# An S4 convolution with a gated linear unit on one core: token normalisation and three copies on GpSimd, and a new written-out order

## Chip, core and metric

The kernel runs on one core of a Trainium2 chip. The metric is the device time in microseconds of one execution, median of the runs. Engines are named as in the profile: PE is TensorE (matrix products, with PEld its weight loads), DVE is VectorE, ACT is ScalarE, POOL is GpSimd, SP is SyncE, whose queue here only issues DMAs.

## What is computed

The input u has 2048 tokens of 512 channels, in bf16. It is normalised over the channels; the normalised xn goes through two branches, and u and both results are added.

```python
xn = (u - mean) / sqrt(var + 1e-5)            # per token, 512 channels
K  = real(einsum("dn,dnl,dn->dl", C, exp(dt * A * l), dt * B))   # 128 modes, l = 0 .. 2047
y  = irfft(rfft(pad(xn)) * rfft(pad(K))) + xn * Dskip            # long convolution over tokens
g  = (sigmoid(xn @ w_gate) * (xn @ w_up)) @ w_down               # 512 -> 1792 -> 512
out = u + y + g
```

## The kernel before

**Tiles and stages.** Tokens lie on 128 partitions, 16 tokens to a partition (index i, 0 to 15; "token" below means one such slice of 128 tokens by 512 channels). Channels are done in two halves b of 256. The gated unit works in eight groups of two tokens. Its stages for a group: the transposed input xnT, products with W into PSUM tiles pg and pu (L824), a sigmoid on ACT into hT (L881), a product on DVE (L883), and the down products po (L829).

**The normalisation** (`layernorm`, L449 on). DVE takes statistics per token (bn_stats, L454), in three batches: tokens 0 and 1, 2 and 3, and 4 to 15. For each batch it forms mean and variance, POOL takes the square root of the variance as a power (sd, L503), and DVE takes the reciprocal (rinv, L479) and the bias nb (L480). Each token is then normalised by one instruction: L483 on DVE, or L487 on ACT. Tokens 4 to 15 are all on ACT in the kernel before. Groups 0 and 1 are transposed by PE (L493) and copied out of PSUM; groups 2 to 7 by DMA transposes on SP's queue, one a token. The spectrum of xn (pzx, L787) needs all tokens.

**The convolution kernel K** is built without 2048 exponentials per mode. `params` computes the first exponentials of a half by exponential and sine at four time scales (ACT and DVE, tiles wp and wq, f32), squares them (L609 to L620), and copies them as bf16 into H and gm by four copies of 128x1024 (L622, here called the H and gm copies). `hlevels` then fills the 21 rows of H by complex products on DVE (L667 to L670, L683 to L686), and `level` fills the 32 rows of G by doubling: five levels, each of two products (L642 into a scratch tile tB, L643 into G) and two sums (L644, L645). All of that is DVE work with both operands in SBUF, done once per half for H and twice per half for G (a quarter of the channels each). PE multiplies G with H (pk, L729), ACT or DVE evicts to ks, and DMAs through scratch memory in HBM (kt_scr, then kf) spread K over time steps. The spectra of K (pzk, L807) and xn go through scratch as well (zk_scr, z_scr), are transformed (px, pkf, L952), multiplied (XX, L972 on DVE, either straight from PSUM or after an eviction by ACT, L973), and transformed back (pv, L961, v_scr; py, L1000).

**What sets the order.** Every step is a task of a plan with an engine, a planned duration in us and an optional alternative engine (`alt`). The order of all 919 tasks is written out as a tuple ORDER, the tasks that take their alternative as OTHER, and the PSUM buffer of each PSUM tile as SIDE. `emit` (L206 on) only follows these: an engine executes its tasks in the order of ORDER, and planned durations have no effect on the chip, except through the ORDER that was made with them. DMAs are issued by SP's queue or, by OTHER, by POOL's.

Of the kernel before, what the change touches and what calls it, by code (L numbers as in the profile page):

```python
# [13 lines left out]
ACT = mybir.ActivationFunctionType  # L14
# [15 lines left out]
ND = 256  # L30
# [187 lines left out]
class _Kernel:  # L218
# [230 lines left out]
    def layernorm(self):  # L449
        nc, add, s, xn = self.nc, self.p.add, self.small, self.xn  # L450
        v = nc.vector
# [30 lines left out]
        def norm(i):  # L482
            v.tensor_scalar(out=xn[:, i, :], in0=self.acc[:, i, :], scalar1=s["m_f"][:, i:i + 1], scalar2=s["rinv"][:, i:i + 1],  # L483
                            op0=ALU.subtract, op1=ALU.mult)

        def norm2(i):
            nc.scalar.activation(out=xn[:, i, :], in_=self.acc[:, i, :], func=ACT.Identity, scale=s["rinv"][:, i:i + 1],  # L487
                                 bias=s["nb"][:, i:i + 1])
# [10 lines left out]
        for lo, hi in ((0, 2), (2, 4), (4, 16)):  # L499
            rk = {0: 2, 2: 4, 4: 10}[lo]  # L500
# [3 lines left out]
                out=s["sd"][:, lo:hi], in0=s["ve"][:, lo:hi], in1=s["half"][:].to_broadcast([128, hi - lo]), op=ALU.pow), [r],  # L504
                    rk + 0.5 * (hi - lo))
            r = add("DVE", 0.4, lambda lo=lo, hi=hi: rstd(lo, hi), [r], rk + 0.5 * (hi - lo))
            for i in range(lo, hi):
                self.norm[i] = add("DVE", 0.4, lambda i=i: norm(i), [r], rk + 0.5 * (hi - lo) + 0.1 + 4 * max(0, i - lo - 3),
                                   alt=("ACT", 0.83, lambda i=i: norm2(i)) if i >= 2 else None)
        self.turns = []  # L510
        for g in range(NGRP):
            rk = max(3, 27 * g + 4)
            xT = self.sb([128, KT, GT * 128], "xnT", 4)
            self.xnT.append(xT)
            if g > 1:
# [7 lines left out]
                    take=[pt])  # L523
# [6 lines left out]
    def params(self, b):  # L530
        nc, add, s = self.nc, self.p.add, self.small
# [90 lines left out]
        cp = lambda o, i, **kw: A_(1.03, lambda: act(out=o(), in_=i(), func=ACT.Identity), **kw)  # L622
# [11 lines left out]
    def level(self, T, nq, n, m, after, rk, own):  # L634
# [6 lines left out]
        cost = lambda k: 0.085 + k * sz / 1920  # L641
# [4 lines left out]
        if n < 8:  # L646
            return [self.p.add("DVE", sum(cost(x[0]) for x in ops), lambda: [x[1]() for x in ops], after, rk, take=[tB], use=own)]
# [5 lines left out]
    def hlevels(self, b):  # L653
# [4 lines left out]
        def lv(src, dst, n, m, after, step=1, to=1, each=0):  # L658

            tB = self.sb([128, 2, 2048], "tB", 1)  # L660
            cost = 0.085 + n * ND / 1920
# [10 lines left out]
            return [self.p.add("DVE", 6 * cost - 0.17, go, after, rk, take=[tB], use=own)]  # L672
# [335 lines left out]
    def store(self):  # L1008
# [46 lines left out]
OTHER = (  # L1055
# [6 lines left out]
SIDE = ("03212320310203120132303322221230100130130221102302112132313110301233311013013232321031200130121323212010200021"  # L1062
        "2133132321331232320221202010301313131020021113202321231210120232030333311003002")
# [35 lines left out]
```

## Time and profile before

| | us |
|---|---|
| median of 3 runs | 237.17 (236.57 to 238.12) |
| the profiled execution | 236.26 |
| its span, first to last instruction | 234.5 |
| PE busy | 212.6 (91% of the span), 2149 matrix products |
| DVE busy | 203.8 (87%), 302 instructions |
| ACT busy | 170.3 (73%), 213 instructions |
| POOL busy | 49.1 (21%), 80 instructions |

All durations are of the one profiled execution. Lengths of neighbouring instructions overlap a little, so that a DVE product listed with 0.68 us advances its queue by about 0.60. The granted TensorE clock was 0.998 of full speed. Lines are those of the kernel before; in the changed file they are one further on from L509 up.

### The profile page before, as it was taken

To read this page: it belongs to the slowest core of one execution; us is meant where nothing else is said; L and a number is where in the kernel's file an instruction comes from. 1 tells how busy PE (TensorE), PEld (TensorE's weight loads), DVE (VectorE), ACT (ScalarE), POOL (GpSimd) and SP (SyncE) were. 2 spreads that over 40 slices of the span, in tenths; PEclk is the share of its full clock that TensorE was granted. 3 is DMA by queue.
4 is the path that set the end of the run, shared out by engine and by line. 5 is a ranking of instruction groups with operands and counts; after the bars stand their busy time and mean duration, and the time that the engine had idled before them with its cause. 6 is when DMAs were issued, how large, how long until landed. Compare 5 with 4: busy or idle time off the path is not lost.

```text
span 234.5 us, 5353 instructions
## 1 busy us (share of the span) xinstructions
PE 212.6 (91%) x2149; PEld 147.8 (63%) x2169; DVE 203.8 (87%) x302; ACT 170.3 (73%) x213; POOL 49.1 (21%) x80
## 2 busy tenths in 40 slices
PE   3798999987989979999989999999989995999993
PEld 1386887466568757564868489557656553677641
DVE  3999999899999999999999999369997789885672
ACT  3399999899989959983976184655888878784400
POOL 2400001400002100025002010562453432422031
PEclk9999999999999999999999999999999999999999
DMA  6999900405030530276996865499589997976946
GB/s 174 286 334 350 303 9 0 130 19 136 20 92 3 126 60 1 36 239 157 275 265 186 283 150 171 93 213 244 195 269 312 264 336 232 278 266 179 286 164 224
DMA packets 51963, 43.16 MB, mean 184 GB/s; under 512 B 20113, under 2 KB 44722, under 8 KB 51682
## 3 DMA queue, kind: packets, MB, share of 16 engines
q1 hardware_dynamic: 47218, 30.07, 45.9%
q0 software_dynamic: 4304, 12.54, 17.3%
q8 instruction: 17, 0.28, 0.5%
q10 hardware_dynamic: 416, 0.20, 0.3%
q14 instruction: 8, 0.07, 0.1%
HBM read 25.86 MB, written 15.37 MB: 176 GB/s over the span
## 4 chain that ended last, share of the span: by engine, by line
DVE 42%; PE 38%; ACT 8%; DMA 8%; issue 2%; POOL 1%; SPq 0%; ACTq 0%; DVEq 0%
PE po L829 9%; PE pg L824 8%; PE pu L824 6%; DVE tB L642 6%; DVE G L643 6%; DMA H<-z_scr 3%; DVE G L644 3%; PE pkf L952 3%; DVE G L645 3%; DMA G<-v_scr 3%; DVE stats L454 3%; PE pv L961 2%; PE py L1000 2%; PE pzk L807 2%; PE pk L729 2%
## 5 line engine op out<-in xcount | busy, mean ns | idle before, releaser
L824 PEld LDWEIGHTS <-W 128*128 128x128 bf16 x896 | 86.3, 98 | 22.6 <-issue 8.8
L824 PE MATMUL pg<-xnT,W 128*128 128x256 bf16 x504 | 61.3, 273 | 3.3 <-ACT hT L358 1.2
L824 PE MATMUL pu<-xnT,W 128*128 128x256 bf16 x392 | 47.6, 273 | 1.6 <-DVE xnT L359 1.3
L972 DVE TENSOR_TENSOR XX<-pkf,x 128x1024 bf16<-128x1024 f32 x22 | 26.4, 1221 | 7.9 <-PE pkf L952 4.6
L829 PE MATMUL po<-wd,hT 128*128 128x512 bf16 x134 | 31.4, 379 | 0.4 <-issue 0.2
L884 ACT ACTIVATE ub<-pu 128x1024 bf16<-128x1024 f32 x18 | 18.6, 1032 | 8.7 <-PE pu L824 5.7
L829 PEld LDWEIGHTS <-hT 128*128 128x128 bf16 x140 | 13.5, 98 | 15.6 <-issue 0.6
L881 ACT ACTIVATE hT<-pg 128x1024 bf16<-128x1024 f32 (+1 forms) x16 | 14.7, 917 | 10.9 <-PE pg L824 8.9
L642 DVE TENSOR_TENSOR tB<-G,gm 128x256 bf16<-128x256 bf16 (+4 forms) x20 | 19.6, 980 | 0.3 <-ACT G L704 0.2
L643 DVE TENSOR_TENSOR G<-G,gm 128x256 bf16<-128x256 bf16 (+4 forms) x20 | 19.6, 979 | 0.1
L358 ACT ACTIVATE zs<-pzx 128x1024 bf16<-128x1024 f32 x16 | 16.3, 1039 | 3.9 <-PE pzx L787 3.9
L1004 DVE TENSOR_TENSOR acc<-py,acc 128x1024 bf16<-128x1024 f32 x8 | 9.7, 1220 | 5.9 <-PE py L1000 5.9
L952 PEld LDWEIGHTS <-w 64*64 64x64 bf16 x384 | 9.2, 106 | 8.5 <-issue 4.9
L358 ACT ACTIVATE G<-pv 128x1024 bf16<-128x1024 f32 x13 | 13.1, 1028 | 1.4 <-PE pv L961 1.3
L454 DVE BATCH_NORM_STATS2 stats<-acc 128x6 f32<-128x512 bf16 x16 | 10.5, 682 | 4.0 <-DMA acc<-in_A_u_dram 4.0
L729 PE MATMUL pk<-H,G 128*128 128x84 bf16 x256 | 11.0, 199 | 3.2 <-DVE G L645 1.8
L729 PEld LDWEIGHTS <-G 128*128 128x128 bf16 x256 | 10.2, 96 | 4.6 <-DVE G L645 2.1
L350 POOL DMA_DIRECT2D kf<-kt_scr x14 | 7.8, 563 | 24.1 <-DMA kt_scr<-ks 22.3
L829 PE MATMUL po<-wd,hTb 128*128 128x512 bf16 x54 | 12.6, 379 | 0.1
L973 ACT ACTIVATE XX<-pkf 128x1024 bf16<-128x1024 f32 x10 | 10.1, 1021 | 3.4 <-PE pkf L952 3.4
L358 ACT ACTIVATE x<-px 128x1024 bf16<-128x1024 f32 x10 | 10.2, 1027 | 3.3 <-PE px L952 3.2
L350 POOL DMA_DIRECT2D kt_scr<-ks x5 | 3.7, 736 | 42.6 <-ACT ks L358 42.6
(146 smaller groups left out, 372.2 us busy)
## 6 DMA issues: line engine op xcount, KB each, us to landing
z_scr<-zs SPq DMA_DIRECT2D x13, 256.0 KB, 2.4
zk<-zk_scr SPq DMA_DIRECT2D x11, 256.0 KB, 4.7
v_scr<-G SPq DMA_DIRECT2D x9, 256.0 KB, 3.8
v_scr<-G POOLq DMA_DIRECT2D x7, 256.0 KB, 4.0
W<-in_B_w_up_dram SPq DMA_DIRECT2D x3, 512.0 KB, 5.7
acc<-in_A_u_dram SPq DMA_DIRECT2D x3, 512.0 KB, 8.9
W<-in_B_w_gate_dram SPq DMA_DIRECT2D x3, 512.0 KB, 9.6
zk_scr<-zks SPq DMA_DIRECT2D x6, 256.0 KB, 2.7
```

The costliest lines, as they stand in the source:

```text
L350: go = lambda e: lambda: q[e].dma_start(out=out(), in_=in_(), **(dict(transpose=True) if transpose else {}))
L358: return self.p.add("ACT", 0.17 + n / 1190, lambda: nc.scalar.activation(out=dst(), in_=src(), func=ACT.Identity), after, rank, alt=("DVE" ...
L454: v.bn_stats(out=s["stats"][:, i, :], in_=self.acc[:, i, :])
L642: ops = [(2, lambda: tt(out=tv(), in0=l, in1=mb(1), op=ALU.mult), [], [tB], []), (2, lambda: tt(out=o, in0=l, in1=mb(0), op=ALU.mult), [], ...
L643: (2, lambda: tt(out=o, in0=l, in1=mb(0), op=ALU.mult), [], [], []),
L729: nc.tensor.matmul(o, G[:, q, r].rearrange("p g c -> p (g c)"), H[:, r, :, 4 * (CQ * c + q):4 * (CQ * c + q) + 4], start=r == 0, stop=r == 1)
L824: nc.tensor.matmul(p[:, lo + n, :], W[:, i, kt, k * 128:(k + 1) * 128], xT[:, kt, :], start=kt == 0, stop=kt == KT - 1)
L829: nc.tensor.matmul(po[:, jj, :], hT[:, k, jj * 128:(jj + 1) * 128], wd[:, k, :], start=k == 0, stop=k == FT - 1 and self.outs[i // GT].eng ...
L881: e1 = add("ACT", 0.17 + n * 256 / 1190, lambda hk=hk, n=n, pg=pg: nc.scalar.activation(out=hk(), in_=pg[:, 0:n, :], func=ACT.Sigmoid), mg ...
L884: e2 = add("ACT", 0.17 + n * 256 / 1190, lambda uk=uk, pk=pk: nc.scalar.activation(out=uk(), in_=pk(), func=ACT.Identity), mu + [e1], rk + ...
L952: nc.tensor.matmul(p[o:o + 64, par, h, :], self.w3[i:i + 64, w, 64 * g:64 * g + 64], z[i:i + 64, 2 * h + c, :], start=True, stop=True, til ...
L972: prod = lambda xo=xo, x1=x1, src=None: nc.vector.tensor_tensor(out=xo(), in0=src(), in1=x1[:, 0], op=ALU.mult)
```

## The change

Three things in the code, and a new order.

Tokens 4 to 15 have POOL as their alternative instead of ACT, and all twelve take it. The four H and gm copies of each half get POOL as an alternative, and three of the eight take it: in the first half the H copy of wp, in the second half the H and the gm copy of wq. The planned durations of the G and H operations are set anew; these only enter the planner.

```diff
-        def norm(i):
-            v.tensor_scalar(out=xn[:, i, :], in0=self.acc[:, i, :], scalar1=s["m_f"][:, i:i + 1], scalar2=s["rinv"][:, i:i + 1],
+        def norm(i, e=v):
+            e.tensor_scalar(out=xn[:, i, :], in0=self.acc[:, i, :], scalar1=s["m_f"][:, i:i + 1], scalar2=s["rinv"][:, i:i + 1],
                             op0=ALU.subtract, op1=ALU.mult)
...
-                                   alt=("ACT", 0.83, lambda i=i: norm2(i)) if i >= 2 else None)
+                                   alt=("POOL", 0.9, lambda i=i: norm(i, nc.gpsimd)) if i >= 4 else ("ACT", 0.83, lambda i=i: norm2(i)) if i >= 2 else None)
...
-        cp = lambda o, i, **kw: A_(1.03, lambda: act(out=o(), in_=i(), func=ACT.Identity), **kw)
+        cp = lambda o, i, **kw: A_(1.03, lambda: act(out=o(), in_=i(), func=ACT.Identity),
+                                 alt=("POOL", 1.35, lambda: nc.gpsimd.tensor_copy(out=o(), in_=i())), **kw)
...
-        cost = lambda k: 0.085 + k * sz / 1920
+        cost = lambda k: 0.15 + k * sz / 1920
...
-            return [self.p.add("DVE", sum(cost(x[0]) for x in ops), lambda: [x[1]() for x in ops], after, rk, take=[tB], use=own)]
+            return [self.p.add("DVE", 0.49 + 6 * sz / 1920, lambda: [x[1]() for x in ops], after, rk, take=[tB], use=own)]
...
-            cost = 0.085 + n * ND / 1920
+            cost = 0.49 + 6 * n * ND / 1920
...
-            return [self.p.add("DVE", 6 * cost - 0.17, go, after, rk, take=[tB], use=own)]
+            return [self.p.add("DVE", cost, go, after, rk, take=[tB], use=own)]
...
 ORDER = (
...
 OTHER = (
...
 SIDE = (
```

ORDER, OTHER and SIDE are replaced as a whole. Read against the order before, the main differences are these. On POOL the first H copy stands ahead of the twelve-token power, then eleven norms with the load of Dskip among them, two issues of the ks dump, the twelfth norm and the two copies of the second half; POOL issues 68 DMAs instead of 63. On DVE the fourth G level of the first quarter comes ahead of the large H products of the first half (L683), where it came behind them; the two xnT copies of groups 0 and 1 go to ACT, the first of them behind three of the four exponentials; of the 32 XX products, 17 instead of 22 are taken straight from PSUM, and 15 instead of 10 after an eviction by ACT. In the frequency stage the issues of single z_scr, zk_scr and v_scr transfers are spread otherwise over SP and POOL. The matrix products on PE are the same, in an order that differs in places by some microseconds of work.

More of the change, by code (lines that the diff above doesn't have):

```diff
@@ L1014 @@
 ORDER = (
[40 rows of a table removed]
-OTHER = (
[6 rows of a table removed]
-SIDE = ("03212320310203120132303322221230100130130221102302112132313110301233311013013232321031200130121323212010200021"
-        "2133132321331232320221202010301313131020021113202321231210120232030333311003002")
[40 rows of a table added]
+OTHER = (
[6 rows of a table added]
+SIDE = ("00223310031202133211133201212012233113012333030201121231330032030211323001321203100021200130123310312021210303"
+        "1333303133203112112210231032302323132102231221212233021002311313003023210211003")
 @with_exitstack
```

92 rows, old and new, of tables (ORDER, OTHER) are left out of this document.

## The prediction

> **What bounds the kernel now.** I read the windows first, ten microseconds each: the window, then busy time of PE, PE weight loads, DVE, ACT and POOL (counts in brackets), then clock, DMA share and GB/s.
>
> ```profile
> 30.00:40.00 10.00, 9.95 (x89) 8.50 (x88) 9.83 (x30) 10.00 (x12) 0.00 (x0) 1.00 0.01 3
> 40.00:50.00 10.00, 9.21 (x50) 4.81 (x50) 9.12 (x17) 9.06 (x17) 3.83 (x3) 1.00 0.30 86
> 50.00:60.00 10.00, 8.73 (x78) 7.42 (x77) 9.90 (x15) 9.97 (x13) 0.00 (x0) 1.00 0.35 93
> 60.00:70.00 10.00, 9.36 (x95) 5.36 (x95) 9.90 (x15) 9.25 (x18) 0.00 (x0) 1.00 0.21 54
> 190.00:200.00 10.00, 7.43 (x165) 4.57 (x167) 9.43 (x11) 8.68 (x10) 2.36 (x5) 1.00 0.84 257
> sum 234.50, PE 212.60 PEld 147.79 DVE 203.82 ACT 170.34 POOL 49.11; mean PE 9.24 PEld 6.43 DVE 8.86 ACT 7.41 POOL 2.14
> ```
>
> From 30 to 70 us three engines are nearly full at once and POOL is empty. So ACT has something to gain from giving work away there, and DVE has nothing to spare: 9.90 of 10 us in two of the windows. Then the chain that ended last (start, length, what), and the wait of PE that tells who leads.
>
> ```profile
> 28.10 1.79 DVE stats L454 x3
> 59.83 2.20 DVE tB L642
> 121.88 1.23 DVE G L645
> 123.15 2.55 PE pk L729 x63
> 189.12 8.06 DMA H<-z_scr
> 215.73 6.72 DMA G<-v_scr
> 227.83 3.04 PE po L829 x14
> ```
>
> ```profile
> PE pk L729 <- DVE G L645: 1.8, 2, 0.9
> ```
>
> Between 28 and 123 us all long pieces of the chain are DVE's; behind 123 us they are PE's, with two DMA waits. PE waits for the last G level before it can start pk, twice, 0.9 us at the longest. So a microsecond added to DVE's queue ahead of 123 us arrives at PE whole, and a microsecond taken from ACT there arrives only where DVE waits for ACT. PE's 212.6 busy of 234.5 us leave 21.9 us in all, which caps any gain.
>
> **What leaves ACT.** Rows: line, engine, operation, tiles, shapes, count, busy time, mean ns.
>
> ```profile
> L487 ACT ACTIVATE xn<-acc,nb,rinv 128x512 bf16<-128x512 bf16 x12 | 9.2, 809 | 0.9 <-DVE nb L480 0.9
> L622 ACT ACTIVATE H<-wq 128x1024 bf16<-128x1024 f32 x2 | 2.2, 1084 | 0.0
> ```
>
> Twelve norms at 0.81 us and three copies at 1.08 us are 9.7 + 3.2 = 12.9 us of ACT time. I book it at nothing: the chain there is DVE's, and what DVE could wait for from ACT is a part of the 0.1 or 0.2 us that it stands idle in each full window (0.9 us from 40 to 50). If ACT were the leader after all, PE's waits for ACT's hT would be the gain; that belongs to the rival below.
>
> **What arrives on POOL, and whether it costs DVE.** In the changed order POOL does the first H copy, the power of the twelve-token variance, eleven norms in a row (with a small constant's load among them), two issues of the ks dump, the twelfth norm, then the two copies of the second half of D. DVE runs beside them almost without a pause: behind the twelve-token rinv and nb come four G operations, two hTb products, two more G levels and the H levels, nearly all products or sums with both operands in SBUF. The trace has no norm or copy on POOL, but shows POOL and DVE side by side (start, length):
>
> ```profile
> 0.95 0.51 POOL L432 MEMSET g<- 128x512 bf16 x1
> 9.48 0.74 POOL L503 TENSOR_TENSOR sd<-ve,half 128x2 bf16<-128x2 bf16 x1 [2.54 <-DVE m_f L475]
> 10.17 0.31 POOL L429 MEMSET H<- 128x256 bf16 x1
> 10.42 0.31 POOL L430 MEMSET H<- 128x256 bf16 x1
> 40.02 2.73 POOL L503 TENSOR_TENSOR sd<-ve,half 128x12 bf16<-128x12 bf16 x1 [28.74 <-DVE ve L474]
> ```
>
> ```profile
> 9.70 0.43 DVE L579 TENSOR_TENSOR wp<-wq 128x256 f32<-128x256 f32 x1
> 10.16 0.72 DVE L582 TENSOR_SCALAR wp<-wp 128x256 f32<-128x256 f32 x1
> 11.25 0.69 DVE L359 COPY xnT<-pt 128x1024 bf16<-128x1024 bf16 x1
> 11.86 0.28 DVE L582 TENSOR_SCALAR wp<-wp 128x256 f32<-128x256 f32 x1
> 41.59 0.42 DVE L645 TENSOR_TENSOR G<-G,tB 128x512 bf16<-128x512 bf16 x1
> 42.78 0.23 DVE L479 RECIPROCAL rinv<-sd 128x12 f32<-128x12 bf16 x1 [0.78 <-POOL sd L503]
> ```
>
> Three readings. The same L582 takes 0.28 us alone and 0.72 us while POOL's two memsets run from 10.17 to 10.73: DVE lost 0.44 us to 0.56 us of POOL work. L579, two operands in SBUF, kept its 0.43 us inside the two-column power, which has almost nothing to read. And the twelve-column power, begun while DVE was in a run of G operations, ended at 42.75, that is 0.74 us behind the end of the last of them (41.59 + 0.42 = 42.01), the length that it has alone with two columns. Either POOL stood blocked for two microseconds, or ten more columns cost 0.2 us each; the trace can't tell.
>
> The Trainium skill, "SBUF — State Buffer", section "Who interferes with whom", says that DVE and GpSimd share a port pair under an exclusive lock held for a whole instruction, and that a DVE instruction with two SBUF inputs contends with a GpSimd instruction that reads SBUF. The stretched L582 agrees for POOL writes; no row here shows it for POOL reads. The Trainium skill, "GPSIMD Engine Reference", section 3.1, has 512 elements in a tight loop at 769 ns; twelve such norms and three copies of 1024 elements at the same rate would hold DVE for an estimated 9.2 + 4.6 = 13.8 us, and the time would be about 248 us.
>
> From rows alone, the price for DVE lies between nothing (L579) and ACT's own lengths, 12 x 0.81 + 3 x 1.08 = 12.9 us. I take the POOL row nearest in size, the memset of 128x512 at 0.51 us, for each norm: 12 x 0.51 = 6.1 us. For a copy of 1024 elements I take twice that, 1.02 us, and count two of the three, because the first runs early, among DVE's bn_stats with their one operand: 2.0 us. Together **+8.1 us**, on the part of DVE's queue that the chain follows.
>
> **What DVE itself gains.** Up to the last G operation the changed order has the same DVE work but for these:
>
> ```profile
> L359 DVE CAST zks<-pzk 128x1024 bf16<-128x1024 f32 x2 | 2.4, 1218 | 0.0
> L883 DVE TENSOR_TENSOR hTb<-hTb,pu 128x1024 bf16<-128x1024 bf16 x1 | 1.2, 1215 | 0.0
> L359 DVE CAST ks<-pk 128x1008 bf16<-128x1008 f32 x2 | 2.3, 1200 | 0.0
> L883 DVE TENSOR_TENSOR hT<-hT,ub 128x1024 bf16<-128x1024 bf16 (+1 forms) x14 | 8.6, 629 | 3.1 <-ACT ub L884 3.1
> L905 DVE TENSOR_TENSOR acc<-po,acc 128x1024 bf16<-128x1024 f32 x3 | 3.7, 1219 | 0.4 <-PE po L829 0.4
> L913 DVE TENSOR_TENSOR acc<-po,acc 128x512 bf16<-128x512 f32 x2 | 1.4, 692 | 1.7 <-PE po L829 1.6
> ```
>
> Away go two xnT copies (2 x 0.69), two zks copies (2.4) and one product from PSUM (1.2): 5.0 us. New are a copy of 128x512 from PSUM (0.69, as L913), a product from SBUF (0.63), a ks copy of 672 elements (0.80 by the 1008-element row) and an accumulation (1.22): 3.3 us. Net **-1.7 us**. The XX products that move from PSUM to SBUF operands (22 to 17 of the direct kind) all lie behind 123 us, where PE leads; I book them at nothing, and ACT's five extra evictions likewise. If DVE or ACT led there, each swap would be 1.22 against 0.68 us on DVE, 2.7 us in all, and 5 x 1.02 = 5.1 us more on ACT.
>
> **The start.** The first xnT copy goes to ACT, behind three of the four exponentials.
>
> ```profile
> 8.97 1.21 ACT L573 ACTIVATE wq<-pz 128x256 f32<-128x256 f32 x4
> 9.18 0.62 PE L493 MATMUL pt<-ident,xn 128*128 128x128 bf16 x8 [0.52 <-DVE xn L483]
> 11.99 6.27 PE L824 MATMUL pu<-xnT,W 128*128 128x256 bf16 x56 [1.32 <-DVE xnT L359]
> L358 ACT ACTIVATE zs<-pzx 128x1024 bf16<-128x1024 f32 x16 | 16.3, 1039 | 3.9 <-PE pzx L787 3.9
> ```
>
> Three exponentials end near 8.97 + 0.9 = 9.9, the transposes at 9.8, a copy of 1024 elements on ACT takes 1.04: PE could begin at 10.9 instead of 12.0. That is worth up to 1.0 us to PE, but DVE's chain from 28 us doesn't begin with it, so the sum has nothing for it.
>
> **The queues.** SP's transposes of group 2 wait for POOL's norms and hold the z_scr stores behind them; PE's group 2 follows.
>
> ```profile
> 44.09 9.77 SPq L350 DMA_TRANSPOSE xnT<-xn  x3
> 49.44 1.91 PE L824 MATMUL pg<-xnT,W 128*128 128x256 bf16 x16 [0.74 <-ACT wq L573]
> ```
>
> The first transpose starts at 44.1 and PE begins group 2 at 49.4: 5.3 us for the pair of norms that it needs and their transposes. I take it that this hides a POOL norm that waits for a DVE operation now and then; it is gone when the pair comes some two microseconds later than now (an estimate from those two times), and then PE stands for the rest. Five more DMA issues on POOL, and the kt_scr issues behind the norms, cost nothing: POOL has 49 busy of 234 us.
>
> **The sum.** The profiled execution took 236.26 us (span 234.5), 0.9 below the median of 237.17. 236.26 + 8.1 - 1.7 = **242.7 us**.
>
> One more row, for ACT's share in PE's waits.
>
> ```profile
> L824 PE MATMUL pg<-xnT,W 128*128 128x256 bf16 x504 | 61.3, 273 | 3.3 <-ACT hT L358 1.2 <-ACT hT L881 1.1 <-ACT wq L573 0.7
> ```
>
> **Rivals.** *POOL is the one that starves* (0.13): if back-to-back DVE instructions keep the port, as the 2.73 us power allows, norms only get in where DVE stops, and in the windows from 50 to 70 us that is 0.2 us. Then group 2 misses its 49.4 us and PE stands until DVE has run out of its G operations, which by the chain is at about 59.83 + 2.20 = 62.0 us: up to 12.6 us lost, a time of up to 248.9, and I take 245 to 249 us. It decides when a POOL norm takes over 2 us. *No clash on reads* (0.30), the other side: POOL fetches ahead as L579 beside the power suggests, DVE keeps its lengths, and DVE's -1.7 and PE's earlier start of 1.0 both hold: 236.26 - 2.7 = 233.6 us. It decides while DVE's G operations stay within a few per cent of their lengths. With ACT's relief added, at most the 3.0 us that PE waits for ACT ahead of pg, 230.6. *Nothing arrives* (0.09): no clash, but PE, 91% busy, only shifts its waits, and the late DMA waits of 8.06 and 6.72 us return in another place: 236 us.
>
> **How the numbers follow.** My own case, DVE held by POOL, has 0.48; its own range goes from two thirds of the price (236.26 + 5.4 - 1.7 = 240.0) to ACT's lengths (236.26 + 12.9 - 1.7 = 247.5). Slower by over 1% (above 239.5; 1% is about what a measurement of this kernel can tell from no change) takes the two slower cases, 0.61. Faster by over 1% (below 234.8) takes nearly all of the no-clash case, 0.27; the rest, 0.12, lies between. Range: 232.0 for the no-clash case with half of ACT's relief, 249.0 for the starved case.
>
> **What would show it.** DVE's lengths for the G operations of equal form, or the gaps in front of them, longer between 43 and 65 us than elsewhere; POOL norms nearer 1 than 0.5 us; the last G operation of the last level behind 128 us instead of 123. Were it at 121 to 122 us with DVE lengths unchanged, the price of +8.1 is wrong and the no-clash rival holds. If the norms on POOL (L483) show gaps of several microseconds between norms and PE waits for xnT near 50 us, it is starvation. If the last G operation is in time and the end still late, the cause lies in the reordered stage behind 123 us, which I booked at nothing.

## The result and the profile after

The changed kernel takes 250.52 us (median of four runs, 249.29 to 250.96), the kernel before beside it 237.64 (four runs, 236.57 to 239.26), a ratio of 1.053, 95% interval 1.045 to 1.060. It is slower, by twice what was forecast, and outside the predicted range. The profiled execution took 250.96 us, with a span of 249.2. Here and below, ratios are of undisturbed runs, medians of all. The line that the changed file has more comes at L623, so lines up to L622 have the same number in both files and later ones are one further on.

First the page's busy times, which answer to the last line of the windows before.

```profile
PE 217.2 (87%) x2169; PEld 150.6 (60%) x2169; DVE 205.1 (82%) x300; ACT 167.6 (67%) x206; POOL 93.5 (38%) x100
```

As shares of the span, no engine is fuller than before except POOL. PE has 4.6 us more for the same work, and it idles 32.0 us instead of 21.9. So the time is in waits. The chain that ended last, the pieces that matter (start, length, what):

```profile
127.75 1.14 DVE G L645
...
128.94 2.59 PE pk L730 x64
...
177.36 7.83 DMA zk_scr<-G
...
185.29 1.24 DVE G L359
...
191.53 6.21 DMA zk<-zk_scr
...
207.95 11.04 DMA v_scr<-G
...
219.11 1.23 DVE G L359
220.39 1.92 PE pv L962 x30
222.31 3.53 PE pg L825 x16
```

The pk stage that waits for the last G operation starts at 128.94 instead of 123.15: 5.8 us of the loss are there by then, where the prediction has 6.4. But the span grew by 14.7, so 8.9 us are lost behind it, where the prediction has nothing. Twice the chain leaves a store (zk_scr<-G, v_scr<-G) for a DVE eviction into G (L359); the first time it comes to PE by two more transfers, the last of them zk<-zk_scr, the second time at once. The waits of the changed kernel name the same links (who for whom: sum, times, longest):

```profile
PE pg L825 <- DMA xnT<-xn: 5.0, 2, 2.8
PE pv L962 <- DVE G L359: 4.9, 2, 4.7
DVE G L359 <- DMA v_scr<-G: 4.8, 1, 4.8
PE px L953 <- DVE G L359: 3.2, 2, 2.9
DVE G L359 <- DMA zk_scr<-G: 3.2, 1, 3.2
```

The fourth and the fifth row are one event, so are the second and the third: DVE may not overwrite a slot of G before the store out of it has landed, and PE stands behind DVE. In the kernel before no eviction waits for a store. (In the changed kernel one more does, on ACT: zks L358 for zk_scr<-zks, 2.6 us. It stays in m1 below, with 2.2 us, where the late loss is gone.) The windows (span, PE busy, weight loads, DVE, ACT, POOL, clock, DMA share, GB/s) show what that does to PE, first that of the kernel before:

```profile
200.00:220.00 20.00, 19.61 (x247) 14.65 (x242) 15.09 (x15) 11.32 (x12) 4.90 (x7) 1.00 0.81 249
```

```profile
200.00:220.00 20.00, 13.44 (x269) 9.45 (x269) 13.92 (x14) 14.41 (x16) 7.12 (x10) 0.98 0.77 230
220.00:230.00 10.00, 9.61 (x89) 6.61 (x89) 6.15 (x7) 2.96 (x3) 0.00 (x0) 0.69 0.37 107
```

PE idles 6.6 us of the first window, where the kernel before has 0.4, and in the second it is busy but at a granted clock of 0.69.

Then POOL, and DVE beside it. POOL's norms as a group (busy, mean ns), and DVE's timeline from 43 to 54 us:

```profile
L483 POOL TENSOR_SCALAR xn<-acc,m_f,rinv 128x512 bf16<-128x512 bf16 x12 | 37.6, 3138 | 0.5 <-DVE rinv L479 0.4
```

```profile
43.75 0.72 DVE L645 TENSOR_TENSOR G<-G,tB 128x512 bf16<-128x512 bf16 x1
44.39 0.41 DVE L646 TENSOR_TENSOR G<-G,tB 128x512 bf16<-128x512 bf16 x1
...
45.69 0.87 DVE L579 TENSOR_TENSOR wp<-wq 128x256 f32<-128x256 f32 x1
...
47.09 0.66 DVE L582 TENSOR_SCALAR wp<-wp 128x256 f32<-128x256 f32 x1
47.78 0.87 DVE L583 TENSOR_TENSOR wp<-wp 128x256 f32<-128x256 f32 x1
...
50.84 0.28 DVE L582 TENSOR_SCALAR wp<-wp 128x256 f32<-128x256 f32 x1
```

A norm takes 3.14 us on POOL, six times the memset that priced it, and by the view of the tile xn (shortest, median and longest in ns) up to 6.57:

```profile
L483 POOL TENSOR_SCALAR xn<-acc,m_f,rinv x12: 2072/2635/6567, 42.4 to 80.1; 128x512 bf16<-128x512 bf16 x12
```

DVE's operations beside them are longer by some 0.4 us each, but only now and then one of them: the sum of 128x512 takes 0.72 and the next one, of the same form, 0.41 (both have 0.42 in the kernel before); L579 has 0.87 instead of 0.43, L582 0.66 and then 0.28.

### The profile page after: what moved, and what is told of

Its sections match the earlier page's. It is cut to its first block, busy times and chain, and to the rows that moved or that the text cites. A ratio compares the mean times of both kernels' runs of the same rounds, so it can differ in the third digit from the quotient of the medians.

```text
span 249.2 us, 5380 instructions
## 1 busy us (share of the span) xinstructions
PE 217.2 (87%) x2169; PEld 150.6 (60%) x2169; DVE 205.1 (82%) x300; ACT 167.6 (67%) x206; POOL 93.5 (38%) x100
## 4 chain that ended last, share of the span: by engine, by line
DVE 39%; PE 29%; DMA 13%; issue 11%; ACT 4%; POOL 2%; SPq 1%; POOLq 0%; DVEq 0%; ACTq 0%
PE po L830 8%; PE pg L825 7%; DVE tB L643 6%; PE pu L825 5%; DMA v_scr<-G 4%; DVE G L644 4%; DVE G L645 4%; DMA zk_scr<-G 3%; DVE G L646 3%; DMA zk<-zk_scr 2%; PE py L1001 2%; PE pk L730 2%; DVE G L359 2%; PE pkf L953 2%; DVE hTb L884 2%
## 5 line engine op out<-in xcount | busy, mean ns | idle before, releaser
L825 PE MATMUL pg<-xnT,W 128*128 128x256 bf16 x504 | 63.9, 282 | 8.7 <-DMA xnT<-xn 5.0
L483 POOL TENSOR_SCALAR xn<-acc,m_f,rinv 128x512 bf16<-128x512 bf16 x12 | 37.6, 3138 | 0.5 <-DVE rinv L479 0.4
L973 DVE TENSOR_TENSOR XX<-pkf,x 128x1024 bf16<-128x1024 f32 x17 | 20.6, 1220 | 9.6 <-PE pkf L953 8.0
L882 ACT ACTIVATE hT<-pg 128x1024 bf16<-128x1024 f32 (+1 forms) x16 | 14.7, 922 | 15.4 <-PE pg L825 15.4
L358 ACT ACTIVATE zs<-pzx 128x1024 bf16<-128x1024 f32 x16 | 16.1, 1024 | 7.7 <-issue 5.7
L358 ACT ACTIVATE G<-pv 128x1024 bf16<-128x1024 f32 x11 | 11.1, 1035 | 11.2 <-PE pv L962 11.2
L974 ACT ACTIVATE XX<-pkf 128x1024 bf16<-128x1024 f32 x15 | 15.2, 1024 | 3.4 <-PE pkf L953 3.0
L953 PEld LDWEIGHTS <-w 64*64 64x64 bf16 x384 | 9.6, 106 | 12.9 <-issue 11.9
L358 ACT ACTIVATE x<-px 128x1024 bf16<-128x1024 f32 x14 | 14.2, 1026 | 3.6 <-PE px L953 3.6
L962 PE MATMUL pv<-XX,w 64*64 64x256 bf16 x256 | 10.6, 292 | 5.6 <-DVE G L359 4.9
L350 POOL DMA_DIRECT2D zk<-zk_scr x10 | 7.5, 756 | 18.8 <-DMA zk_scr<-zks 12.3
L359 DVE CAST G<-pv 128x1024 bf16<-128x1024 f32 x5 | 6.1, 1220 | 9.1 <-DMA v_scr<-G 4.8
L503 POOL TENSOR_TENSOR sd<-ve,half 128x2 bf16<-128x2 bf16 (+1 forms) x3 | 3.9, 1311 | 25.3 <-DVE ve L474 18.7
```

The costliest lines, as they stand in the source:

```text
L358: return self.p.add("ACT", 0.17 + n / 1190, lambda: nc.scalar.activation(out=dst(), in_=src(), func=ACT.Identity), after, rank, alt=("DVE" ...
L483: e.tensor_scalar(out=xn[:, i, :], in0=self.acc[:, i, :], scalar1=s["m_f"][:, i:i + 1], scalar2=s["rinv"][:, i:i + 1], op0=ALU.subtract, o ...
L825: nc.tensor.matmul(p[:, lo + n, :], W[:, i, kt, k * 128:(k + 1) * 128], xT[:, kt, :], start=kt == 0, stop=kt == KT - 1)
L882: e1 = add("ACT", 0.17 + n * 256 / 1190, lambda hk=hk, n=n, pg=pg: nc.scalar.activation(out=hk(), in_=pg[:, 0:n, :], func=ACT.Sigmoid), mg ...
L953: nc.tensor.matmul(p[o:o + 64, par, h, :], self.w3[i:i + 64, w, 64 * g:64 * g + 64], z[i:i + 64, 2 * h + c, :], start=True, stop=True, til ...
L973: prod = lambda xo=xo, x1=x1, src=None: nc.vector.tensor_tensor(out=xo(), in0=src(), in1=x1[:, 0], op=ALU.mult)
```

## The experiments

Seventeen kernels ran, each beside the kernel before on the same chip. All but e6, which was no comparison of times, are in the table. It has the ratio to the kernel before with its 95% interval, and from the one profiled execution of each the start of that pk stage and the time from there to the end of the span ("behind", span minus start). It is the last two columns that tell early from late.

| run | ratio | pk at | behind |
|---|---|---|---|
| before | 1 | 123.15 | 111.4 |
| changed kernel | 1.053 [1.045, 1.060] | 128.94 | 120.3 |
| e1_norms_act | 1.037 [1.030, 1.044] | 124.92 | 117.3 |
| e3_order_only | none, 239.73 to 247.68 us | 125.16 | 112.7 |
| e4_old_order_pool_norms | 1.048 [1.040, 1.055] | 134.50 | 111.5 |
| e5_spare_pool_norms | 1.027 [1.020, 1.033] | 128.99 | 110.8 |
| n1_norms_dve | 1.020 [1.015, 1.025] | 126.98 | 110.4 |
| c1_copies_pool | 1.015 [1.009, 1.020] | 125.77 | 110.8 |
| h1_old_early_new_late | 1.017 [1.012, 1.023] | 122.99 | 114.3 |
| h2_new_early_old_late | 1.007 [1.003, 1.011] | 125.12 | 111.3 |
| e7_late_loads | 1.028 [1.024, 1.033] | 125.13 | 116.9 |
| l1_new_order_old_queues | 1.035 [1.029, 1.041] | 126.28 | 116.3 |
| l2_new_order_old_evictions | 1.045 [1.041, 1.050] | 125.32 | 119.3 |
| m1_after_wide_rings | 1.022 [1.016, 1.028] | 128.84 | 110.8 |
| m2_order_only_wide_rings | 1.007 [1.004, 1.010] | 125.23 | 110.5 |
| m3_before_wide_rings | 1.002 [0.999, 1.004] | 123.16 | 110.8 |
| m4_v_ring | 1.032 [1.024, 1.040] | 129.55 | 111.6 |
| m5_zk_ring | 1.044 [1.036, 1.051] | 129.02 | 117.4 |

**The changed order without the norms, or without any work, on POOL.** Both keep the changed order. e1 has the norms on ACT again (in OTHER as before, with ACT as their alternative); e3 has the three copies back on ACT as well.

```diff
-                                   alt=("POOL", 0.9, lambda i=i: norm(i, nc.gpsimd)) if i >= 4 else ("ACT", 0.83, lambda i=i: norm2(i)) if i >= 2 else None)
+                                   alt=("ACT", 0.83, lambda i=i: norm2(i)) if i >= 2 else None)
```

> The changed kernel with the twelve norms back on ACT, at the places that the new order gives them; the three copies stay on POOL. If the late norms on POOL are the whole cause, the time falls by all that was lost, to 236 to 239 us, and the last G operation before pk ends near 123 us. If the new order itself is slow behind 129 us, only the part lost ahead of that comes back: 5 to 6 us, a time of 244 to 246 us, with the waits for v_scr and zk_scr still there.

> The changed kernel with norms and the three copies all on ACT: the new order alone. If the copies matter, it differs from the one with only the norms moved back by 1 to 3 us; if they are hidden, by less than 1 us. If the order is as good as the old one, 235 to 239 us; if it is the source of the loss behind 129 us, 243 to 247 us.

e1 took 244.81 us (244.04 to 246.75), e3 245.09 (239.73 to 247.68). So the norms on POOL account for 5.7 us of the changed kernel by the medians, 3.7 by the ratios (1.053 to 1.037), and the larger part is in the order itself, with nothing on POOL. e3's four runs lie so far apart that it has no interval; its profiled run is its fastest, and behind pk it is 1.4 us slower than the kernel before where e1 is 5.9 slower. Something late differs from run to run.

DVE's busy time up to the pk stage, from the windows of these kernels, takes the early part to pieces. Before, changed, norms on ACT (e1), order alone (e3):

```profile
0.00:123.15 123.15, 116.39 (x208) 1.00 0.52 144
```

```profile
0.00:128.94 128.94, 122.07 (x207) 0.99 0.48 135
```

```profile
0.00:124.92 124.92, 116.95 (x207) 1.00 0.49 140
```

```profile
0.00:125.16 125.16, 115.05 (x207) 1.00 0.50 137
```

The same 207 instructions take DVE 122.07 us with norms and copies on POOL, 116.95 with the copies alone there and 115.05 with neither: twelve norms cost it 5.1 us (0.43 each), three copies 1.9. Without them the new order has 1.3 us less DVE work than the old (116.39). Idle in the changed kernel is 6.9 us, before 6.8; the four terms make 5.1 + 1.9 - 1.3 + 0.1 = 5.8, the whole delay of pk. In e1 DVE idles 8.0 us and in e3 10.1, with more waits for ACT (tB for ACT's eviction into G is 0.9 in e1 and 1.9 in e3): in the new order the move gives back some 3 us of DVE's time, 1.1 by the norms and 2.1 by the copies, but it is the new order that needs it.

**The norms in the order before.** e4 puts the twelve norms on POOL in the order of the kernel before; e5 leaves them on ACT and has POOL do twelve equal ones that nobody reads (extra work), one beside each; n1 has DVE do them all, by leaving the twelve out of OTHER.

```diff
+        junk = self.const.tile([128, D], BF, name="junk")
+        def spare(i):
+            nc.gpsimd.tensor_scalar(out=junk[:], in0=self.wd[:, i - 4, :], scalar1=s["m_f"][:, i:i + 1], scalar2=s["rinv"][:, i:i + 1],
+                                    op0=ALU.subtract, op1=ALU.mult)
...
-                                   alt=("ACT", 0.83, lambda i=i: norm2(i)) if i >= 2 else None)
+                                   alt=("ACT", 0.83, lambda i=i: [norm2(i), spare(i)][0] if i >= 4 else norm2(i)) if i >= 2 else None)
```

> The kernel before, its order untouched, with tokens 4 to 15 normalised by POOL. If POOL is starved beside DVE, norms take 2 to 3 us or more each as in the changed kernel, PE waits for xnT near 50 us, and the time is 242 to 247 us. If the new order is the whole cause, it stays at 236 to 239 us. If DVE were held instead, DVE's operations between 43 and 70 us would be longer by 6 us in sum and the time 243 us with no wait for xnT.

> The kernel before with twelve more norms on POOL that nobody reads (from the down weights into a tile of their own, each behind the ACT norm of its token in the order); the real norms stay on ACT. It parts the hold on DVE from the lateness of the norms. If the loss is lateness, the spare norms are long (2 to 3 us) but the time rises by 2 us at most; if DVE is held by each, the time rises by 5 to 8 us and DVE's operations beside them are longer by as much.

> The kernel before, its order untouched, with tokens 4 to 15 normalised by DVE, at 0.40 us each as its first four. The aligned traces say that a POOL norm lengthens one DVE instruction by 0.4 us. If that hold and what follows from it is what the spare norms cost (6.1 us), norms on DVE itself cost about the same, 4 to 6 us, a time of 240 to 243 us, and PE has no wait for xnT. If the spare norms cost something else on POOL (its queue, the late kt_scr issue), norms on DVE cost clearly less, 238 us or under.

e5 (242.22 us, 241.64 to 244.4) isolates what a norm on POOL does to DVE: nobody waits for the spare ones, and the kernel still loses 6.1 us. Up to pk DVE is busy for 4.9 us more than before, and it waits 0.9 us for ACT's eviction into G, which it doesn't in the kernel before; that is the 5.8 us by which pk comes later. DVE's timeline in e5, then in the kernel before (L690 there is L684):

```profile
43.50 0.79 DVE L585 TENSOR_TENSOR wp<-wq 128x256 f32<-128x256 f32 x1
...
44.81 0.95 DVE L689 TENSOR_TENSOR H<-H 128x1536 bf16<-128x1536 bf16 x1
45.68 1.36 DVE L690 TENSOR_TENSOR tB<-H 128x1536 bf16<-128x1536 bf16 x1
```

```profile
43.45 0.43 DVE L579 TENSOR_TENSOR wp<-wq 128x256 f32<-128x256 f32 x1
...
45.27 0.95 DVE L684 TENSOR_TENSOR tB<-H 128x1536 bf16<-128x1536 bf16 x1
```

Set side by side over the whole run, 13 DVE instructions are longer by over 0.1 us, by 0.17 to 0.50 us, most of them near 0.4, and by 4.8 us in sum, for twelve norms. n1 (240.50 us, 239.21 to 240.93) says what this is worth. Its group of norms on DVE, all sixteen tokens:

```profile
L483 DVE TENSOR_SCALAR xn<-acc,m_f,rinv 128x512 bf16<-128x512 bf16 x16 | 6.2, 406 | 0.0
```

A norm takes DVE 0.41 us, so a norm on POOL costs it at least as much as doing the work. Up to pk DVE is busy for 3.8 us more than before in n1 and for 4.9 in e5, and the time grows by 4.7 us in n1 and by 6.1 in e5.

e4 (247.62 us, 246.53 to 248.99) adds what POOL's slowness costs: 5.4 us more than e5. PE's timeline in e4:

```profile
51.63 0.38 PE L787 MATMUL pzx<-xn,s1p 128*128 128x512 bf16 x1 [3.13 <-POOL xn L483]
54.16 3.57 PE L824 MATMUL pg<-xnT,W 128*128 128x256 bf16 x16 [2.16 <-DMA xnT<-xn]
```

PE waits for the norm itself, then for its transpose, and then does 16 products in 3.57 us that take 1.91 elsewhere. DVE stands behind it: up to pk it idles 12.4 us, in the kernel before 6.8. Behind pk e4 and e5 are as the kernel before: all of this is early.

**One norm alone.** Three norms that nobody reads (extra work), behind POOL's first memsets, while DVE waits for its first token and then, from 3.8 us on, does its first bn_stats.

```diff
-nc.gpsimd.memset(self.zero, 0.0)], rank=-1001)
+nc.gpsimd.memset(self.zero, 0.0), *[nc.gpsimd.tensor_scalar(out=junk[:], in0=self.zero, scalar1=s["half_pi"][:], scalar2=s["half_pi"][:],
+    op0=ALU.subtract, op1=ALU.mult) for _ in range(3)]], rank=-1001)
```

> The kernel before with three spare norms of 128x512 on POOL right behind its first memsets, while DVE still waits for its first token. It measures a POOL norm with nobody beside it. If the three microseconds of the norms are waiting for DVE, a norm alone takes 0.6 to 1.0 us; if a norm is simply slow on POOL, 2 us or more.

Its time (one run, 244.6 us) says nothing of norms beside DVE's products, since the three hold up the start: POOL's load of ident behind them goes out at 7.97 us, and DVE waits 2.6 us for the first power. The group of the three norms in e6 (min, median, max in ns):

```profile
L433 POOL TENSOR_SCALAR junk<-g,half_pi x3: 2070/2075/2085, 1.6 to 5.9; 128x512 bf16<-128x512 bf16 x3
```

Alone, a norm takes POOL 2.08 us, with a spread of 15 ns; the last of the three, beside bn_stats, is no longer than the first. The mean of 3.14 beside DVE is 1.06 us more, and the spare ones of e5 go from the length alone to three times that:

```profile
L489 POOL TENSOR_SCALAR junk<-wd,m_f,rinv x12: 2074/3442/6459, 43.9 to 105.7; 128x512 bf16<-128x512 bf16 x12
```

**The copies alone**, in the order before: the three of them get POOL as in the change, and their numbers go into OTHER.

```diff
-        cp = lambda o, i, **kw: A_(1.03, lambda: act(out=o(), in_=i(), func=ACT.Identity), **kw)
+        cp = lambda o, i, **kw: A_(1.03, lambda: act(out=o(), in_=i(), func=ACT.Identity),
+                                 alt=("POOL", 1.35, lambda: nc.gpsimd.tensor_copy(out=o(), in_=i())), **kw)
```

> The kernel before, its order untouched, with the three H and gm copies on POOL. If a copy holds DVE as a norm does, about 0.4 us each and once, 236 to 238 us, hardly to be told from before; at the 1.02 us a copy of the prediction, with two of three counted, 238.5 to 239 us.

238.85 us (238.1 to 241.38) against 235.78, some 3 us, and pk comes 2.6 us later. DVE's timeline of c1 beside the three copies:

```profile
20.74 1.86 DVE L612 TENSOR_TENSOR wq<-wq,sr 128x1024 f32<-128x1024 f32 x1
...
90.69 2.13 DVE L884 TENSOR_TENSOR hTb<-hTb,ub 128x1024 bf16<-128x1024 bf16 x2
92.74 1.25 DVE L618 SCALAR_TENSOR_TENSOR H<-wq 128x256 bf16<-128x256 f32 x1
```

In the kernel before these take 1.23, 1.29 and 0.42 us: 2.3 us more together, and each of the three copies costs, the first one too. In the changed order, by the windows above, it is 1.9; the times of e1 and e3 are too scattered to show it.

**Early part, late part.** h1 takes the first 548 tasks of ORDER from the kernel before and the rest in the changed order, h2 the first 506 from the changed order and the rest as before. Norms and copies stay on ACT.

```diff
-ORDER = <all 919 tasks in one order>
+ORDER = <the first 548 (h2: 506) of one order, then the remaining tasks in the sequence of the other>
```

> All norms and copies on ACT; the first 548 tasks in the old order with the old engines and PSUM buffers (through the last pk but for a few), the rest in the new order with its own. If the new order loses in the stage behind 129 us, this is as slow as the new order alone, 242 to 247 us; if it loses ahead of it, 235 to 238 us.

> All norms and copies on ACT; the first 506 tasks in the new order (through the three quarters of G ahead of the last), the rest in the old order; three PSUM buffers had to be chosen anew at the seam. If the new order loses late, 235 to 239 us; if it loses early, 241 to 246 us; with the early part's 2 us of delay at the last pk as measured, 238 to 239 us.

240.80 us (239.06 to 241.6) and 238.19 (237.22 to 239.4) against 236.71. The new late part costs 4.1 us even when it starts on time, the new early part 1.5.

**What it is in the late part.** Three edits of the changed order with norms and copies on ACT. e7 moves the four kf<-v_scr loads from POOL's queue to SP's, behind the fourth store of v_scr; l1 gives the DMAs behind pk the queues that they had before; l2 gives the evictions and XX products behind pk their engines of before.

```diff
 OTHER = (
-    <choices of the changed kernel behind the pk stage>
+    <those of the kernel before: for DMAs (l1), for all but DMAs (l2)>
```

> The new order with all norms and copies on ACT, but the four kf loads of the first half's v_scr go from POOL's queue to SP's, behind the fourth v_scr store of the second half, so that they no longer stand beside the stores on the DMA engines. If the 10 to 11 us that a v_scr store takes to land there are the late loss and the source of the scatter, the time falls from 245 us to 238 to 241 us and scatters less; if the stores are slow for another cause, it stays at 244 to 246 us.

> The new order with norms and copies on ACT, but with every DMA behind the last pk on the queue (SP or POOL) that it has in the old kernel. If the late loss comes from the new spread over the two queues, the time falls from 245 us to 237 to 240 us; if it comes from the order or from the split of evictions, it stays at 243 to 247 us.

> The new order with norms and copies on ACT, but with every eviction and product behind the last pk on the engine (ACT or DVE) that it has in the old kernel, DMAs as in the new one. If the new split of evictions (five more XX on ACT) makes the late loss, 237 to 240 us; if queues or order do, 243 to 247 us or more.

243.31 us (242.35 to 243.82), 246.77 (243.89 to 250.96) and 246.55 (246.31 to 247.1): no recovery. Neither the old queues nor the old split of the evictions brings the time back, and fewer loads beside the store help a little at most. What is left is the sequence. Both rows in which DVE's eviction into G waits for a store stand in the changed kernel, in e1 and in e7; in the profiled runs of e3 and l1 the one for zk_scr stands alone, 2.0 and 2.9 us. In l2 neither stands: with the evictions on other engines its chain goes through evictions and XX products on ACT and DVE, and it loses 7.9 us behind pk all the same. What holds l2 was not followed up, so l2 doesn't show that the split has no part in the loss.

**The slots of G.** The staging for v_scr has four slots of 128x1024 in G, that for zk_scr in the second half four more. By the time of the stores gm and ks are idle and have room for two slots each. m1 is the changed kernel with six slots in both rings, m2 the same with norms and copies on ACT (e3), m3 the kernel before with the wider rings; m4 and m5 are the changed kernel with one ring widened.

```diff
-                zs = self.late("zks1", [4, ND], (self.G[:], 4, 4)) if b else ...
+                zs = self.late("zks1", [4, ND], (self.G[:], 4, 4), (self.gm[:], 0, 2)) if b else ...
...
-            vs = self.late("vs", [4, ND], (self.G[:], 0, 4))
+            vs = self.late("vs", [4, ND], (self.G[:], 0, 4), (self.ks[:], 0, 2))
```

> The changed kernel, with six slots instead of four for the staging ring of v_scr (two more in ks) and six for the ring of zk_scr of the second half (two more in gm). Theory 'reuse of slots': DVE's eviction no longer waits for v_scr<-G (4.8 us) and zk_scr<-G (3.2 us), PE's waits for DVE's eviction (4.7 and 2.9 us) and the slow products behind them go: 250.5 - 6 to 8, so 242.5 to 245. Rival 'the transfers themselves or the order of PE': the wait moves on to the loads, 249 to 251.

> The changed order alone (norms and copies on ACT) with the wider rings. Theory 'reuse of slots': the scatter of 239.7 to 247.7 shrinks to its lower end or below, 237 to 240. Rival: as before, about 245.

> Control: the kernel before with the wider rings. Its trace shows no eviction into G that waits for a store, so both theories expect no change, within 1 us of the kernel before; a gain here would say that the rings cost something in any order.

> The changed kernel with the v_scr ring alone widened to six slots. If the two waits cost in proportion to what they show (4.8 us here with 1.7 us of slow products behind it, 3.2 us at the other), this brings some 6 of the 8.9 us: 244 to 246. If all hangs on the zk_scr ring, 249 to 251.

> The changed kernel with the zk_scr ring of the second half alone widened to six slots. By the waits some 3 of the 8.9 us: 247 to 248. If an earlier zk_scr also lets the v_scr stores start early enough, up to all of it, 242 to 244.

In the changed kernel this is the late cause. m1 takes 241.64 us (241.33 to 242.12) where the changed kernel takes 250.52; by the ratios, which allow for the chip, that is 0.031 of 236.2, or 7.2 us. m2 takes 237.92, and its ten runs lie between 237.35 and 239.16 where e3's four were spread over 8 us. m3 stays where it was, 236.38 against 236.16, so the rings cost the order before nothing. Behind pk both m1 and m2 are at the kernel before. The rest of m1's loss is early: m1 and m2 differ by 0.015 in the ratio, 3.5 us, and by 3.6 us in the start of pk, which is what norms and copies on POOL cost, and m2 starts pk 2.1 us later than the kernel before. The v_scr ring alone brings 4.9 us (1.053 to 1.032), the zk_scr ring alone 2.1 (to 1.044); the sum is 7.0 of 7.2. The waits had said it: the two events cost DVE 4.8 and 3.2 us. With the v_scr ring alone (m4) the one wait is gone and the other stays; with the zk_scr ring alone (m5) it is the reverse:

```profile
PE px L953 <- DVE G L359: 2.2, 2, 1.9
DVE G L359 <- DMA zk_scr<-G: 2.2, 1, 2.2
```

```profile
PE pv L962 <- DVE G L359: 4.7, 2, 4.5
DVE G L359 <- DMA v_scr<-G: 4.6, 1, 4.6
```

Why does the new sequence run into the slots? For v_scr, the chain of the changed kernel shows the store before it is issued:

```profile
203.29 0.43 ACT G L358
...
204.97 2.00 ACT G L358 x2
206.98 0.36 SPq L350
...
207.39 0.50 SPq L350
```

and POOL's timeline what is issued around it:

```profile
206.34 2.80 POOL L350 DMA_DIRECT2D G<-v_scr  x4 [4.68 <-DVE XX L973]
209.13 0.78 POOL L350 DMA_DIRECT2D v_scr<-G  x1
209.90 2.81 POOL L350 DMA_DIRECT2D kf<-v_scr  x4
```

By the written order, the store that lands at 219.0 belongs to the eviction that ended at 204.2. On SP's queue it stands behind the stores of two later evictions, the last of which ended at 206.97, so it goes out at 207.95, nearly 4 us late; then it needs 11 us, with eight loads of 256 KB issued from 206.3 to 212.7. The fourth eviction behind it wants the same slot at 214.3 and gets it at 219.1. In m1 that store takes as long (10.84 us in its chain), but the slot is wanted later: an eviction on ACT waits 1.1 us for it, and PE's pv no longer stands behind it.

```profile
ACT G L358 <- DMA v_scr<-G: 1.1, 1, 1.1
```

For zk_scr the sequence was not followed up in this way.

No kernel that was run beats the kernel before.

## Why the prediction was wrong

**Right, in kind and nearly in size: all that lies ahead of pk.** POOL's hold on DVE was booked at 6.1 us for the norms and 2.0 for the copies; DVE's busy time has 5.1 and 1.9. DVE's own work was booked at -1.7; it is -1.3. The norms' agreement is in part luck, since 0.51 us stood for the length of a norm on POOL, which is 3.14. So is that of the copies: two were counted at 1.02 us and the first at nothing, "among DVE's bn_stats", but the three cost about 0.6 each, the first one beside a product (L611, 1.74 us instead of 1.22). The sum was +6.4 at the last G operation; it came 5.8 late, behind 128 us as the prediction said that it would. With the late cause taken out (m1) the changed kernel takes 241.64 us, beside a forecast of 242.7. ACT's 12.9 us booked at nothing was right for the order before: up to pk DVE idles 6.8 us there and as much in n1, where ACT has no norms. In the new order the relief is needed to keep DVE's idle time at 6.9 us, so there too no time is won.

**Wrong, and this is the step that failed:** "Up to the last G operation" was costed, and of what lies behind 123 us the prediction says "where PE leads; I book them at nothing". It weighed the engines and evictions there, but not the slots in which evictions are staged. PE led there only while no eviction had to wait for its slot; the trace of before has no such wait, and the new sequence has two on DVE. They cost 7.2 us by the ratios, 9.5 in the two profiles (120.3 against 110.8 behind pk). The evidence was within reach: four slots, landings of v_scr stores of up to 7.8 us before, and the changed file has the order of evictions, stores and loads. The prediction named that stage as the place to look if the end came late with G in time; G was late as foreseen, and the stage failed besides.

**Wrong in its price, though the term came out:** a norm on POOL takes 2.08 us alone and 3.14 here, not "nearer 1 than 0.5". The memset row priced two things with one number. What DVE loses (0.43) was near it; how long POOL needs was four times it. The Trainium skill, "GPSIMD Engine Reference", section 3.1, with its 769 ns for 512 elements in a tight loop, is too low for a norm: 2075 ns alone. And "SBUF — State Buffer", section "Who interferes with whom", has the port pair locked for a whole instruction; the trace agrees that each engine holds up the other, but DVE lost 0.4 us to a norm of 2.08 and not the length of it.

**The starved rival** was true on POOL and false on the clock. Its sign, a norm of over 2 us, doesn't tell it from the other cases, since a norm takes 2.08 alone. But norms beside DVE came up to 6.57 us long, and PE stood 5.0 us for xnT. The cover of the prediction, gone "when the pair comes some two microseconds later", was gone, and in the order before that costs 5.4 us (e4 against e5). In the changed order it costs nothing that can be seen: m1 has the same 5.0 us of waiting and ends 5.2 us behind the kernel before, about what DVE's last G operation is late (5.7 us at pk). The rival of no clash on reads falls by the lengths of L579, L583 and L645; that nothing arrives, by the result.

## What to carry to other kernels

When an order changes, list for each ring of staging slots how many evictions lie between an eviction and the next into its slot, and where its store stands in its queue: a ring that never waits in one order can stall the leading engine in the next, and two more slots in idle memory may undo it. Price a moved operation twice, by its length on the new engine and by what it takes from its neighbour, and measure the first alone, with the neighbour idle. A sum that stops at the stage it can see needs a term, or at least a range, for the stage behind.

## What the runs showed of the hardware

A norm on GpSimd takes 2.08 us alone and up to 6.57 beside VectorE's run of products, while VectorE loses about 0.4 us to each, at least as much as when it does the norm itself (0.41).

A short idle of PE costs more than itself. In the changed kernel's timeline of PE:

```profile
52.27 3.45 PE L825 MATMUL pg<-xnT,W 128*128 128x256 bf16 x16 [2.77 <-DMA xnT<-xn]
55.55 1.91 PE L825 MATMUL pu<-xnT,W 128*128 128x256 bf16 x16
```

Sixteen products behind an idle time of 2.77 us take 3.45 us, the next sixteen 1.91; behind the 4.68 us at 220 us it is 3.60, and the 32 of pv ahead of them take 1.92 us, where 32 take 1.04 at 192 us. Windows of one microsecond (span, PE busy, clock, DMA share, GB/s) show half the clock behind both waits, the first time until 55 us, the second until 226 us:

```profile
53.00:54.00 1.00, 1.00 (x7) 0.50 0.41 154
223.00:224.00 1.00, 1.00 (x7) 0.50 0.08 14
```

So the 4.7 us wait cost some 7.2 (an estimate: 4.7 + 1.7 + 0.9). The Trainium skill, "TensorE: Matmul & The Clock Gate", section "What's actually happening", gives half the clock after an idle window of some 3.4 us; the granted 0.50 agrees with half the clock, but here 2.77 us of waiting were enough, behind 28 products of po in 6.21 us and two more in 0.60.
